# K-features times V in the two halves of the array's columns, with the normalizer's sums added on GpSimd

## The chip, the cores and the metric

The kernel runs on one core of one Trainium2 chip. The metric is the device time of one execution in microseconds; of several executions the median is given. The core's engines are TensorE (matrix products; "PE" in the profile, with "PEld" for the loads of its stationary operand), VectorE (DVE), ScalarE (ACT), GpSimd (POOL) and SyncE (SP), which issues the transfers.

## The reference

Inputs are float32. The attention has 8 batches, 8 heads, 576 tokens and 64 values per head; each head's queries and keys become 256 positive features, and numerator and denominator are linear in them. The result, 4608 tokens by 512, goes through a gated feed-forward with 1536 hidden values.

```python
def phi(x):
    proj = np.einsum('bhsd,df->bhsf', x, w_phi)             # 128 features
    proj = proj - np.max(np.abs(proj), axis=-1, keepdims=True)
    return np.concatenate([np.exp(proj), np.exp(-proj)], axis=-1)
q_p, k_p = (phi(q), phi(k))
kv = np.einsum('bhsf,bhsd->bhfd', k_p, v)
z = np.sum(k_p, axis=2)
num = np.einsum('bhsf,bhfd->bhsd', q_p, kv)
den = np.einsum('bhsf,bhf->bhs', q_p, z)[..., None] + 1e-06
x = num / den                                               # heads side by side: 4608 x 512
out = (sigmoid(x @ w_gate) * (x @ w_val)) @ w_out
```

The change concerns `kv` and `z`: for each head, the sum over tokens of features times values, and the sum over tokens of the features alone.

## The kernel before, in words

The attention runs over 32 pairs of heads (`steps`, 8 batches of 4 pairs). For one pair:

- `load_q`, `load_kv`: transfers of the pair's queries, keys and values. Values come as `vx`, 128 tokens by ten blocks (five blocks of tokens, the two heads alternating) by 65 columns: 64 values and a column of ones, which `layout` puts there. The last block of a head has only 64 tokens; they lie in the partitions of its own half, with zeros in the other.
- `att_k`: the keys' projections on TensorE into `pp` (L316, L321), in three groups `g` (token blocks 0 and 1 of both heads, blocks 2 and 3, and the last half block); VectorE takes the maximum (L325) and subtracts it (L344), ScalarE takes the two exponentials (L350; L338 for the first four pairs). Then the products with V (L358): for each head and each of five token blocks, 65 stationary columns of `vx` by 256 features, in plain float32, added up in `kvp` (65 partitions, 2 heads, 256 features). Row 64 of `kvp` is the sum of the features, because of the column of ones. ScalarE copies `kvp` to `kvt` (L364), TensorE transposes it in four pieces into `tp` (L367), and ScalarE and VectorE copy that out as `kvh` and `kvl` (`split`, L60 and L61), or in the first eight pairs (`WHOLE`) as `kv` (L370).
- `att_q`: the queries' projections (L397, L403) and, on VectorE, their maximum over the features, which lie across the partitions (L413 to L428).
- `att_num`: the queries' exponentials (L439), their splitting (L446, L447) and the products with `kvh` and `kvl` (L456): 65 rows, the last of which is the denominator. Twice per pair, a half of the tokens each.
- `att_norm`, `att_scale`: the reciprocal of the denominator through memory, the scaling (L484) into `xp` (two buffers), and its transfer to `xscr`.

The feed-forward runs in two parts. Its first five blocks of 128 hidden values (`half_units`: L136 into `gv`, L143 into `acc`) run beside the attention, as units that `fill` releases at 0.7 per slot, four slots per pair. The other seven (`rest_chunks`) run when the attention has ended (L136 into `g` and `v`, L143).

The order of the instructions on each engine is not written by hand: the framework lists them with a timeline simulation of its own when the kernel is built; what stands under `attend` has priority over the rest. Each engine then works through its list in order. Memory on the chip is nearly full, which is why many tiles have one or two buffers. Before the change GpSimd makes the identity matrix at the start, and nothing else.

Of the kernel before, what the change touches and what calls it, by code (L numbers as in the profile page):

```python
# [19 lines left out]
F = 128  # L20
# [10 lines left out]
HS = S // 2  # L31
KVW = D + 1

JA = 5  # feed-forward blocks that run beside the attention
JR = 8  # blocks JA to JR - 1 take the attention's bytes, the others phase 1's
WHOLE = 8  # first pairs: plain float32 products, no splits
DIRECT = 4  # first pairs: K's exponentials straight from PSUM
PRIORITY = 400
RATE, LAG = 0.7, 2  # feed-forward units per slot; slots from x to its first unit


@with_exitstack
def attention_moe(
# [20 lines left out]
        for m in marks:  # L64
            stack.enter_context(tc.issue_after(m.ins))

# [1 line left out]
    weights = {}  # L68

    ebias = const.tile([P, 1], F32, name="ebias")  # L70
    vec.memset(ebias, -896.0 * 2.0**23)

    def from_f64(h, l, raw, mid, sp, nb, name):
        # h: the value cut to 12 bits; l: the other bits as an integer times their unit
        words = raw.rearrange("p (n two) -> p n two", two=2)
        lo, hi = words[:, :, 0], words[:, :, 1]
        top = sp.tile([P, DM], U32, tag="wtop", name="wtop" + name, bufs=nb)
        vec.tensor_scalar(top, hi, 0x7FFFFE00, None, op0=ALU.bitwise_and)
        relu = act.activation(top, top, AF.Relu, bias=ebias, scale=8.0)
        vec.scalar_tensor_tensor(  # L80
            top, hi, 0x80000000, top, op0=ALU.bitwise_and, op1=ALU.bitwise_or
        )
        vec.tensor_copy(h, top.bitcast(F32))
        if mid is None:
            rest, unit = hi, lo
            vec.tensor_scalar(
                hi, hi, 16, 0x01FF0000, op0=ALU.logical_shift_left, op1=ALU.bitwise_and
            )
            vec.scalar_tensor_tensor(
                hi, lo, 16, hi, op0=ALU.logical_shift_right, op1=ALU.bitwise_or  # L90
            )
        else:
            words = mid.rearrange("p (n two) -> p n two", two=2)
            rest, unit = words[:, :, 0], words[:, :, 1]
            vec.tensor_scalar(rest, rest, 0x01FFFFFF, None, op0=ALU.bitwise_and)
        vec.tensor_scalar(unit, top, 0xFF800000, None, op0=ALU.bitwise_and)
        return relu, vec.scalar_tensor_tensor(
            l, rest, 2.0**-36, unit.bitcast(F32), op0=ALU.mult, op1=ALU.mult
        )

    def load_weights(j, m, wp, sp, nb, twice):
        if m == 0:
            wh = wp.tile([P, 3 * DM], F32R, tag=f"wh{j}", name=f"wh{j}")
            wl = wp.tile([P, 3 * DM], F32R, tag=f"wl{j}", name=f"wl{j}")
            weights[j] = (wh, wl)
        wh, wl = weights[j]
        ms = slice(m * DM, m * DM + DM)
        raw = sp.tile([P, 2 * DM], U32, tag="wraw", name=f"wraw{j}_{m}", bufs=nb + 1)
        load, mid = nc.sync.dma_start(raw, w_moe[j, :, m, :].bitcast(U32)), None
        if twice:  # L110
            # the same rows two bytes on: a word then holds the bits below h's
            mid = sp.tile([P, 2 * DM], U32, tag="wmid", name=f"wmid{j}_{m}", bufs=nb)
            nc.sync.dma_start(
                mid[:, : 2 * DM - 1].bitcast(U16),
                w_moe[j, :, m, :].bitcast(U16)[:, 1 : 4 * DM - 1],
            )
        return load, *from_f64(wh[:, ms], wl[:, ms], raw, mid, sp, nb, f"{j}_{m}")
# [135 lines left out]
            xs = nxt  # L253
        out_step(*late)

# [1 line left out]
    with ExitStack() as actx:  # L257
        wp1 = actx.enter_context(tc.tile_pool(name="wp1", bufs=1))
        moe = actx.enter_context(tc.tile_pool(name="moe1", bufs=2))
# [5 lines left out]
        ps_n = actx.enter_context(tc.tile_pool(name="ps_n", bufs=1, space=PSUM))  # L265
        ps_acc = actx.enter_context(tc.tile_pool(name="ps_o", bufs=1, space=PSUM))

        ident = at1.tile([KVW, KVW], F32, name="ident")
        make_identity(nc, ident)
        wk = at1.tile([P, 3 * F], F32, name="wk")  # L270
        nc.sync.dma_start(wk, w_phi)
        wq = at1.tile([P, 2, 3 * F], F32R, name="wq")
# [12 lines left out]
        def load_kv(b, p):  # L285
            n = f"{b}_{p}"
            kx = at.tile([P, 5 * P], F32, tag="kin", name="k" + n)
            nc.sync.dma_start(kx, k[b, p])
            vx = at.tile([P, 10, KVW], F32, tag="vin", name="v" + n)
            nc.sync.dma_start(vx, v[b, p])  # L290
            loaded["kv", b, p] = (kx, vx)

        def att_k(b, p):
            n = f"{b}_{p}"
            kx, vx = loaded.pop(("kv", b, p))
            kvp = ps_kv.tile([KVW, 2, 2 * F], F32, tag="kvp", name="kvp" + n)
            es = []
            whole = b * NP + p < WHOLE
            if not whole:
# [3 lines left out]
            for g in range(3):  # L303
# [38 lines left out]
                else:  # L342
# [6 lines left out]
                    for sg in range(2):  # L349
# [2 lines left out]
                            scale=1.0 - 2.0 * sg,  # L352
                        )
                es.append(e)
            for hd in range(2):
                for t in range(5):
                    slot = 2 * t + hd
                    nc.tensor.matmul(  # L358
                        kvp[:, hd, :], vx[:, slot, :],
                        es[t // 2][:, slot % 4 if t < 4 else 0, :],  # L360
                        start=t == 0, stop=t == 4,
                    )
            kvt = at.tile([KVW, 4, F], F32, tag="kvt", name="kvt" + n, bufs=1)
            act.copy(kvt.rearrange("p a f -> p (a f)"), kvp.rearrange("p a f -> p (a f)"))  # L364
            tp = ps_kv.tile([P, 4, KVW], F32, tag="kvp", name="tp" + n)
            for i in range(4):
                nc.tensor.transpose(tp[:, i, :], kvt[:, i, :], ident)  # L367
            if b * NP + p < WHOLE:
                kv = at.tile([P, 4, KVW], F32, tag="kv", name="kv" + n)
                act.copy(kv, tp)  # L370
                kvs[b, p] = (kv,)
            else:
                kvh = at.tile([P, 4, KVW], F32R, tag="kv", name="kvh" + n)
                kvl = at.tile([P, 4, KVW], F32R, tag="kvl", name="kvl" + n)
                split(kvh, kvl, tp)
                kvs[b, p] = (kvh, kvl)

        def att_q(b, p):
# [53 lines left out]
        def att_num(b, p, hf):  # L432
            n = f"{b}_{p}_{hf}"
            d, ex = qst[b, p]
            cs = slice(hf * HS, hf * HS + HS)
            terms = []
            for sg in range(2):
                e = at.tile([P, 2, HS], F32, tag="eq", name=f"eq{n}_{sg}", bufs=2)
                act.activation(e, d[:, :, cs], AF.Exp, scale=1.0 - 2.0 * sg)  # L439
                if len(kvs[b, p]) == 1:  # L440
                    terms.append([(kvs[b, p][0], e)])
                else:
                    kvh, kvl = kvs[b, p]
                    eh = at.tile([P, 2, HS], F32R, tag="eqh", name=f"eqh{n}_{sg}", bufs=2)
                    el = at.tile([P, 2, HS], F32R, tag="eql", name=f"eql{n}_{sg}", bufs=2)
                    act.copy(eh, e)  # L446
                    late[b, p, hf, sg] = vec.tensor_tensor(  # L447
                        el, e, eh.bitcast(F32), op=ALU.subtract
                    )
                    terms.append([(kvh, eh), (kvl, eh), (kvh, el)])  # L450
            for hd in range(2):
                nm = ps_n.tile([KVW, HS], F32, tag="nm", name=f"nm{n}_{hd}")
                last = len(terms[0]) - 1
                for sg in range(2):
                    for i, (a, x) in enumerate(terms[sg]):
                        nc.tensor.matmul(  # L456
                            nm, a[:, 2 * hd + sg, :], x[:, hd, :],
                            start=sg == 0 and i == 0, stop=sg == 1 and i == last,
                        )
                act.copy(ex[:, hd, cs], nm)  # L460
# [18 lines left out]
        def att_scale(b, p):  # L479
            n = f"{b}_{p}"  # L480
            ex, rb = rbs.pop((b, p))
            xp = at.tile([P, S], F32, tag="xp", name="xp" + n, bufs=2)
            for hd in range(2):
                vec.tensor_tensor(  # L484
                    xp[hd * D : hd * D + D, :], ex[0:D, hd, :], rb[:, hd, :], op=ALU.mult
                )
            t = 0
            while t < S:
                c, o = divmod(b * S + t, CH)
                w = min(CH - o, S - t)  # L490
                nc.sync.dma_start(
                    xscr[c][:, p * CH + o : p * CH + o + w], xp[:, t : t + w]
                )
                t += w
# [104 lines left out]
def layout(inputs):  # L599
    import numpy as np  # L600

    def feature_major(x):
# [5 lines left out]
    kt[:, :, :D, 4 * P : 4 * P + D] = x[:, :, :D, 4 * P :]  # L608
    kt[:, :, D:, 4 * P + D :] = x[:, :, D:, 4 * P :]
    x = inputs["v"].reshape(B, NP, 2, S, D)  # L610
    x = np.concatenate([x, np.ones_like(x[..., :1])], axis=-1)
    vt = np.zeros((B, NP, P, 10, KVW), x.dtype)
    vt[:, :, :, :8] = (
        x[:, :, :, : 4 * P]
        .reshape(B, NP, 2, 4, P, KVW)
        .transpose(0, 1, 4, 3, 2, 5)
        .reshape(B, NP, P, 8, KVW)
    )
    vt[:, :, :D, 8] = x[:, :, 0, 4 * P :]
    vt[:, :, D:, 9] = x[:, :, 1, 4 * P :]  # L620
# [17 lines left out]
```

## Time and profile before

| | us |
|---|---|
| median of 3 executions | 1304.68 |
| lowest, highest | 1303.23, 1305.15 |
| profiled execution, span from first to last instruction | 1307.2 |
| TensorE busy in it | 1269.8 |
| VectorE busy | 877.5 |
| ScalarE busy | 650.7 |
| GpSimd busy | 0.6 |

The profile is of one execution, whose span is given in the table. "L358" is line 358 of the kernel before. In a row of grouped instructions stand the line, the engine, the operation, the program's names for what is written and read, the shapes, the count, the busy time in us, the mean duration of one in ns, and the idle time of the engine ahead of them with what ended it. A matmul's duration is modelled and overlaps its neighbours'; the distance from one start to the next is what it takes of the engine. The chain of waits is followed back from the last instruction, at each step to what released it or to the instruction before it on its engine; a piece of it such as "x10" holds ten instructions one behind the other. In tables by stretch of time, each engine's busy time stands with its number of instructions.

### The profile page before, as it was taken

The numbers are of one execution on the slowest core, as the hardware profiler recorded it, in microseconds if no ns is written. First come the engines' busy times: TensorE is split into PE (matmuls) and PEld (weight loads), VectorE is DVE, ScalarE is ACT, GpSimd is POOL, SyncE is SP. The second block draws the span as 40 slices with busy tenths as digits, with TensorE's granted clock in tenths as the row PEclk, the third lists the DMA queues.
The fourth block names the chain that finished last, engine by engine and source line by source line (L and its number), as shares of the span: only waits on it lengthen the run. The fifth ranks groups of instructions, "written<-read, shape, count | busy, mean of one in ns | idle before, by whom it ended". The sixth has DMA issues, their size and how long they took to land.

```text
span 1307.2 us, 19107 instructions
## 1 busy us (share of the span) xinstructions
PE 1269.8 (97%) x7112; PEld 1070.8 (82%) x7112; DVE 877.5 (67%) x1778; ACT 650.7 (50%) x1416; POOL 0.6 (0%) x6
## 2 busy tenths in 40 slices
PE   7878999999999999999999999999999999999998
PEld 4545788999898989898998988888888888888886
DVE  5777989899899888989866958834343443434333
ACT  5754777777777787777754523322222222222221
POOL 0000000000000000000000000000000000000000
PEclk9988999999999999999999999999999999999999
DMA  5576543233233323332225424313021211202010
GB/s 190 165 216 195 167 131 100 85 107 105 86 115 86 107 84 118 94 108 76 61 69 180 130 78 132 97 65 97 1 97 33 65 50 48 97 1 97 1 65 33
DMA packets 75166, 125.12 MB, mean 96 GB/s; under 512 B 18496, under 2 KB 38080, under 8 KB 75072
## 3 DMA queue, kind: packets, MB, share of 16 engines
q1 hardware_dynamic: 75072, 123.89, 30.7%
q8 instruction: 56, 0.92, 0.3%
q14 instruction: 38, 0.31, 0.1%
HBM read 95.25 MB, written 28.46 MB: 95 GB/s over the span
## 4 chain that ended last, share of the span: by engine, by line
PE 88%; DVE 4%; DMA 4%; ACT 2%; issue 1%; SPq 0%; DVEq 0%; ACTq 0%
PE acc L143 22%; PE gv L136 17%; PE g L136 13%; PE v L136 13%; PE kvp L358 9%; PE nm L456 7%; PE pk L316 3%; PE pq L403 2%; PE pq L397 1%; DMA xs<-xp 1%; DMA q<-q 1%; DMA rb<-den 1%; DMA dn<-ex 1%; ACT ek L338 1%; DMA wraw<-w_moe 1%
## 5 line engine op out<-in xcount | busy, mean ns | idle before, releaser
L136 PE MATMUL gv<-xh,wh 128*128 128x256 f32 x720 | 208.3, 290 | 3.6 <-DVE t L156 3.4
L136 PE MATMUL gv<-xh,wl 128*128 128x256 f32 x720 | 206.5, 287 | 0.0
L136 PE MATMUL gv<-xl,wh 128*128 128x256 f32 x720 | 206.2, 286 | 0.0
L60 ACT CAST hh<-u 128x256 fp32r<-128x256 f32 (+1 forms) x153 | 75.4, 494 | 245.3 <-DVE u L157 245.1
L143 PE MATMUL acc<-wh,hh 128*128 128x512 f32 x432 | 171.3, 397 | 0.7 <-ACT y L187 0.7
L143 PE MATMUL acc<-wl,hh 128*128 128x512 f32 x432 | 169.9, 393 | 0.0
L143 PE MATMUL acc<-wh,hl 128*128 128x512 f32 x432 | 166.1, 394 | 0.1
L358 PE MATMUL kvp<-ek,v 128*65 128x256 f32 x640 | 158.6, 383 | 6.9 <-ACT ek L338 5.3
L155 DVE TENSOR_SCALAR t<-t 128x256 uint32<-128x256 uint32 (+1 forms) x153 | 52.5, 344 | 154.6 <-ACT t L152 153.7
L136 PEld LDWEIGHTS gv<-xh,wh 128*128 128x128 f32 x720 | 137.1, 191 | 10.0 <-DVE t L156 4.7
L136 PEld LDWEIGHTS gv<-xl,wh 128*128 128x128 f32 x720 | 137.0, 190 | 3.3
L136 PEld LDWEIGHTS gv<-xh,wl 128*128 128x128 f32 x720 | 137.0, 190 | 2.3
L358 PEld LDWEIGHTS kvp<-ek,v 128*65 128x65 f32 x640 | 86.6, 138 | 49.4 <-ACT ek L338 9.7
L61 DVE TENSOR_TENSOR hl<-u,hh 128x256 fp32r<-128x256 f32 (+1 forms) x153 | 81.1, 531 | 47.2 <-ACT hh L60 46.1
L152 ACT ACTIVATE t<-g 128x512 f32<-128x512 f32 x63 | 37.6, 597 | 150.0 <-PE g L136 149.8
L156 DVE SCALAR_TENSOR_TENSOR t<-t,v 128x512 f32<-128x512 f32 x63 | 43.3, 687 | 85.6 <-PE v L136 85.4
L136 PE MATMUL g<-xh,wh 128*128 128x512 f32 x252 | 99.0, 393 | 0.0
L136 PE MATMUL v<-xh,wh 128*128 128x512 f32 x252 | 98.6, 391 | 0.0
L136 PE MATMUL g<-xl,wh 128*128 128x512 f32 x252 | 98.6, 391 | 0.0
L136 PE MATMUL g<-xh,wl 128*128 128x512 f32 x252 | 98.5, 391 | 0.0
L136 PE MATMUL v<-xl,wh 128*128 128x512 f32 x252 | 98.3, 390 | 0.0
L136 PE MATMUL v<-xh,wl 128*128 128x512 f32 x252 | 98.2, 390 | 0.0
(91 smaller groups left out, 2533.6 us busy)
## 6 DMA issues: line engine op xcount, KB each, us to landing
wraw<-w_moe SPq DMA_DIRECT2D x36, 512.0 KB, 3.9
xl<-xs SPq DMA_DIRECT2D x36, 512.0 KB, 4.1
v<-v SPq DMA_DIRECT2D x32, 325.0 KB, 3.3
k<-k SPq DMA_DIRECT2D x32, 320.0 KB, 3.1
q<-q SPq DMA_DIRECT2D x32, 288.0 KB, 3.2
rb<-den SPq DMA_DIRECT2D x32, 288.0 KB, 3.8
ys<-y SPq DMA_DIRECT2D x36, 256.0 KB, 2.1
yp<-ys SPq DMA_DIRECT2D x36, 256.0 KB, 4.3
```

Of the source, the lines that this page charges most:

```text
L60: a = act.copy(h, x)
L61: return a, vec.tensor_tensor(l, x, h.bitcast(F32), op=ALU.subtract)
L136: nc.tensor.matmul(o, a[:, ws], x[:, cs], start=i == 0, stop=i == 11)
L143: nc.tensor.matmul(acc, a[:, ts], w[:, ws], start=first and i == 0, stop=last and i == 2)
L152: act.activation(t, g, AF.Tanh, scale=0.5)
L155: vec.tensor_scalar(tu, tu, 0x7FFFFFFF, None, op0=ALU.bitwise_and)
L156: vec.scalar_tensor_tensor(t, t, 1.0, vl, op0=ALU.add, op1=ALU.mult)
L316: nc.tensor.matmul(o, x[:, ts], w, start=t == 0, stop=t == len(terms) - 1)
L338: act.activation(e[:, i, sg * F : sg * F + F], pp[:, i, :], AF.Exp, bias=(mn, mx)[sg][:, i : i + 1], scale=1.0 - 2.0 * sg,)
L358: nc.tensor.matmul(kvp[:, hd, :], vx[:, slot, :], es[t // 2][:, slot % 4 if t < 4 else 0, :], start=t == 0, stop=t == 4,)
L403: nc.tensor.matmul(pp, wq[:, i, 2 * F :], s[:, hd, cs], start=i == 0, stop=i == 1,)
L456: nc.tensor.matmul(nm, a[:, 2 * hd + sg, :], x[:, hd, :], start=sg == 0 and i == 0, stop=sg == 1 and i == last,)
```

## The change

The values lose their column of ones, so a head's product has 64 stationary columns. Head 0's goes to partitions 0 to 63 of `kvp`, head 1's to partitions 64 to 127, of the same 256 columns; the loops over token blocks and heads change places, so that the heads alternate. The sums of the features over the tokens are now made in two steps: GpSimd adds the exponentials of a head's token blocks elementwise into `su` (128 partitions by 2 heads by 256), and two products with a matrix of ones add up the 128 partitions, into the other half of `kvp`, where each of 64 partitions then holds the same sum.

```diff
-        ident = at1.tile([KVW, KVW], F32, name="ident")
+        ident = at1.tile([P, P], F32, name="ident")
         make_identity(nc, ident)
+        ones = at1.tile([P, D], F32, name="ones")
+        vec.memset(ones, 1.0)
...
-            vx = at.tile([P, 10, KVW], F32, tag="vin", name="v" + n)
+            vx = at.tile([P, 10, D], F32, tag="vin", name="v" + n)
...
-            kvp = ps_kv.tile([KVW, 2, 2 * F], F32, tag="kvp", name="kvp" + n)
+            kvp = ps_kv.tile([P, 2, 2 * F], F32, tag="kvp", name="kvp" + n)
...
+            su = at.tile([P, 2, 2 * F], F32, tag="su", name="su" + n, bufs=1)
+            pool.tensor_tensor(su, es[0][:, 0:2, :], es[0][:, 2:4, :], op=ALU.add)
+            for i in (0, 2):
+                pool.tensor_tensor(su, su, es[1][:, i : i + 2, :], op=ALU.add)
             for hd in range(2):
-                for t in range(5):
+                own = slice(hd * D, hd * D + D)
+                pool.tensor_tensor(
+                    su[own, hd, :], su[own, hd, :], es[2][own, 0, :], op=ALU.add
+                )
+
+            for t in range(5):
+                for hd in range(2):
                     slot = 2 * t + hd
                     nc.tensor.matmul(
-                        kvp[:, hd, :], vx[:, slot, :],
+                        kvp[hd * D : hd * D + D, 0, :], vx[:, slot, :],
                         es[t // 2][:, slot % 4 if t < 4 else 0, :],
                         start=t == 0, stop=t == 4,
                     )
-            kvt = at.tile([KVW, 4, F], F32, tag="kvt", name="kvt" + n, bufs=1)
+            for hd in range(2):
+                nc.tensor.matmul(
+                    kvp[hd * D : hd * D + D, 1, :], ones, su[:, hd, :],
+                    start=True, stop=True,
+                )
+            kvt = at.tile([P, 4, F], F32, tag="kvt", name="kvt" + n, bufs=1)
             act.copy(kvt.rearrange("p a f -> p (a f)"), kvp.rearrange("p a f -> p (a f)"))
-            tp = ps_kv.tile([P, 4, KVW], F32, tag="kvp", name="tp" + n)
+            tp = ps_kv.tile([P, 4, P], F32, tag="kvp", name="tp" + n)
             for i in range(4):
                 nc.tensor.transpose(tp[:, i, :], kvt[:, i, :], ident)
+            parts = [
+                (slice(0, D), tp[:, 0:2, :].rearrange("p s (h d) -> p h s d", h=2)),
+                (
+                    slice(D, KVW),
+                    tp[:, 2:4, :].rearrange("p s (h d) -> p h s d", h=2)[:, :, :, 0:1],
+                ),
+            ]
...
-                split(kvh, kvl, tp)
+                for ds, x in parts:
+                    split(kvh[:, :, :, ds], kvl[:, :, :, ds], x)
...
-            xp = at.tile([P, S], F32, tag="xp", name="xp" + n, bufs=2)
+            xp = at.tile([P, S], F32, tag="xp", name="xp" + n, bufs=1)
```

`kv`, `kvh` and `kvl` now have the shape 128 by 2 heads by 2 signs by 65, L456 takes its pieces by head and sign, and `layout` leaves out the column of ones. The order of the tokens in `vx`, the rest of the attention and the feed-forward stay as they are.

More of the change, by code (lines that the diff above doesn't have):

```diff
@@ L362, in att_k @@
                     )
-            kvt = at.tile([KVW, 4, F], F32, tag="kvt", name="kvt" + n, bufs=1)
+            for hd in range(2):
[4 more added lines that the diff above has]
+            kvt = at.tile([P, 4, F], F32, tag="kvt", name="kvt" + n, bufs=1)
             act.copy(kvt.rearrange("p a f -> p (a f)"), kvp.rearrange("p a f -> p (a f)"))
-            tp = ps_kv.tile([P, 4, KVW], F32, tag="kvp", name="tp" + n)
+            tp = ps_kv.tile([P, 4, P], F32, tag="kvp", name="tp" + n)
             for i in range(4):
                 nc.tensor.transpose(tp[:, i, :], kvt[:, i, :], ident)
+            parts = [
[5 more added lines that the diff above has]
+            ]
             if b * NP + p < WHOLE:
-                kv = at.tile([P, 4, KVW], F32, tag="kv", name="kv" + n)
-                act.copy(kv, tp)
+                kv = at.tile([P, 2, 2, KVW], F32, tag="kv", name="kv" + n)
+                for ds, x in parts:
+                    act.copy(kv[:, :, :, ds], x)
                 kvs[b, p] = (kv,)
             else:
-                kvh = at.tile([P, 4, KVW], F32R, tag="kv", name="kvh" + n)
-                kvl = at.tile([P, 4, KVW], F32R, tag="kvl", name="kvl" + n)
-                split(kvh, kvl, tp)
+                kvh = at.tile([P, 2, 2, KVW], F32R, tag="kv", name="kvh" + n)
+                kvl = at.tile([P, 2, 2, KVW], F32R, tag="kvl", name="kvl" + n)
+                for ds, x in parts:
+                    split(kvh[:, :, :, ds], kvl[:, :, :, ds], x)
                 kvs[b, p] = (kvh, kvl)
@@ L456, in att_num @@
                         nc.tensor.matmul(
-                            nm, a[:, 2 * hd + sg, :], x[:, hd, :],
+                            nm, a[:, hd, sg, :], x[:, hd, :],
                             start=sg == 0 and i == 0, stop=sg == 1 and i == last,
@@ L610, in layout @@
     x = inputs["v"].reshape(B, NP, 2, S, D)
-    x = np.concatenate([x, np.ones_like(x[..., :1])], axis=-1)
-    vt = np.zeros((B, NP, P, 10, KVW), x.dtype)
+    vt = np.zeros((B, NP, P, 10, D), x.dtype)
     vt[:, :, :, :8] = (
         x[:, :, :, : 4 * P]
-        .reshape(B, NP, 2, 4, P, KVW)
+        .reshape(B, NP, 2, 4, P, D)
         .transpose(0, 1, 4, 3, 2, 5)
-        .reshape(B, NP, P, 8, KVW)
+        .reshape(B, NP, P, 8, D)
     )
```

## The prediction

> **What bounds the kernel now.** I read the page's parts 1, 2 and 4 first.
>
> ```profile
> span 1307.2 us, 19107 instructions
> PE 1269.8 (97%) x7112; PEld 1070.8 (82%) x7112; DVE 877.5 (67%) x1778; ACT 650.7 (50%) x1416; POOL 0.6 (0%) x6
> PE   7878999999999999999999999999999999999998
> DVE  5777989899899888989866958834343443434333
> PE 88%; DVE 4%; DMA 4%; ACT 2%; issue 1%; SPq 0%; DVEq 0%; ACTq 0%
> PE acc L143 22%; PE gv L136 17%; PE g L136 13%; PE v L136 13%; PE kvp L358 9%; PE nm L456 7%; PE pk L316 3%; PE pq L403 2%; PE pq L397 1%; DMA xs<-xp 1%; DMA q<-q 1%; DMA rb<-den 1%; DMA dn<-ex 1%; ACT ek L338 1%; DMA wraw<-w_moe 1%
> ```
>
> TensorE is 88% of the chain that ended last, and K-features times V (L358) is 9% of it. But 97% and 67% are averages over stages, so I cut the span at 172 us (the eight WHOLE pairs end about there), 694 (attention ends) and 782 (the feed-forward alone). Columns: stretch, length, busy time (instructions) of PE, weight loads, DVE, ACT, POOL.
>
> ```profile
> 0.00:172.00 172.00, 143.27 (x675) 97.70 (x676) 134.20 (x302) 107.47 (x270) 0.60 (x6) 0.95 0.59 185
> 172.00:694.00 522.00, 521.84 (x3596) 469.98 (x3597) 451.09 (x952) 377.47 (x859) 0.00 (x0) 1.00 0.32 94
> ...
> PE gv L136 <- DVE t L156: 1.6, 2, 1.4
> ```
>
> The stage that matters is 172 to 694: 24 pairs in 522 us, 21.75 us each, and TensorE is busy for 521.84. The last line is the longest wait of its matmuls there (1.6 us in all). Nothing else holds the stage, so a microsecond of array time there is a microsecond of the end. VectorE is idle for 522 - 451 = 71 us, 2.96 us a pair: the next bound, not far off. Before 172, TensorE is idle for 29 of 172 us, so there I count array time at half: 24 + 8/2 = **28 pairs' worth**.
>
> **The L358 products.** A busy matmul's duration is not what it costs; its step is. The chain of waits gives the steps of one pair (start, length, piece):
>
> ```profile
> 306.74 1.19 PE gv L136 x10
> ...
> 308.71 0.86 PE kvp L358 x4
> ...
> 310.53 0.86 PE kvp L358 x4
> ...
> 313.40 2.16 PE kvp L358 x10
> ...
> 317.14 0.43 PE kvp L358 x2
> ...
> 321.50 0.24 PE tp L367 x4
> ```
>
> ```profile
> L358 PE MATMUL kvp<-ek,v 128*65 128x256 f32 x640 | 158.6, 383 | 6.9 <-ACT ek L338 5.3 <-ACT ek L350 1.1 <-DMA q<-q 0.4
> L358 PEld LDWEIGHTS kvp<-ek,v 128*65 128x65 f32 x640 | 86.6, 138 | 49.4 <-ACT ek L338 9.7 <-ACT ek L350 2.2 <-issue 1.2
> L367 PE MATMUL tp<-ident,kvt 65*128 65x65 f32 x128 | 13.2, 224 | 0.0
> ```
>
> 2.16/10 = 0.216 us per record. The program has 32 x 10 such products and the trace 640 records: a float32 product is two records, one behind the other. A pair pays 20 x 0.216 = **4.32 us**, in four runs (4, 4, 10, 2 records) with other products between them, since the exponentials come in three groups. Each record takes 0.383 us though the step is 0.216: 0.167 us of its depth lies under its neighbours. The 65-column weight load of 0.138 us is under the step too.
>
> **What the change does to TensorE.**
>
> *Removed by overlap.* The heads' products now use 64 columns each, in two halves, and alternate. No product before the change uses half of the columns, so no row shows whether two run at once; the bounds are a step of 0.216 per record (none) and per two records (full). In favour, from rows: gv takes 256 float32 columns per 0.119 us, so operands can stream at nearly twice L358's rate; two L358 streams would need 0.216 for two, against 2 x 0.119 = 0.238. I take overlap at 0.216.
>
> But the order is head 0 first record, second record, head 1 first, second. The two records of one head use the same half and can't overlap each other. So a run of n records takes n/2 + 1 steps: the first and the last have one half empty.
>
> *Added.* Two products with `ones`: four records. So there are 24. The order by token block makes runs of 8 (first group), 8 (second), 4 (third) and 4 (the sums, which come from GpSimd): 5 + 5 + 3 + 3 = 16 steps, 16 x 0.216 = 3.46. Against 4.32 that is **-0.86 us a pair**. If the third group joins the second (12 records), 15 steps and -1.08.
>
> *Transposes.* 0.24/4 = 0.06 us for 65 columns; 128 columns cost at least that and at most 128/65 of it, 0.118: between 0 and +0.23 a pair. I take **+0.12**, the middle.
>
> *The edges.* Four runs have eight edges between full-width and half-width products. If the array can't hold both kinds at once, the depth that now lies under the neighbour is paid at each edge. Lower bound 0: in the pieces above the edge between kvp and gv costs nothing now. Upper: 0.167 and, if the next weights can't be loaded ahead either, 0.138 more. I take 0.167 at each, the only row that shows the depth: 8 x 0.167 = **+1.34 us a pair**. It decides the sign: the saving is gone from (0.86 - 0.12)/8 = 0.09 us an edge on.
>
> The Trainium skill's page "TensorEngine Tiling (Array Packing)", Key Properties, speaks against the change here: changing the tiling mode, not merely the tile, drains the engine; the same list says that tiles execute in parallel. By that rule the sum is the one with the edges; without it, the one without. No run so far shows which.
>
> Sum for TensorE: -0.86 + 0.12 + 1.34 = +0.60 a pair, x 28 = **+17 us**.
>
> **The other engines.**
>
> ```profile
> masks.py:199 POOL TENSOR_SCALAR_AFFINE_SELECT ident<-ident 65x65 f32<-65x65 f32 x1 | 0.2, 238 | 0.1
> L157 DVE SCALAR_TENSOR_TENSOR u<-u,t 128x512 f32<-128x512 f32 x63 | 43.5, 691 | 5.1
> ...
> 309.42 0.51 ACT L350 ACTIVATE ek<-dk 128x128 f32<-128x128 f32 x2
> ...
> 318.52 0.60 ACT L364 COPY kvt<-kvp 65x512 f32<-65x512 f32 x1
> ```
>
> *GpSimd's adds:* three of 128x512 and two of 64x256. No row shows one. Nearest below: VectorE's 0.69 us for 512 elements; above: GpSimd's own 0.238 us for 65 elements, 1.87 for 512. With half for 256 elements, 4 x 0.69 = 2.8 to 4 x 1.87 = 7.5 us a pair; I take 4 x 1.3 = 5 (middle). What waits is the `ones` product, and in TensorE's order everything behind it. Cover: the third group's exponentials end at 309.42 + 0.51 = 309.9, the last L358 product of that pair at 317.14 + 0.43 = 317.6. Even 7.5 us from about 306, when the first group is there, end at 313.5. The buffers of the exponentials, which GpSimd now holds too, and the one of the sums are wanted again a pair later. Cost 0; if the product is placed where the data are ready instead, up to 3.6 us a pair.
>
> *The copies:* kvt keeps its 512 elements per partition (0.60 us); the tp copies become a long and a small one.
>
> ```profile
> L335 DVE TENSOR_SCALAR mn<-mx 128x4 f32<-128x4 f32 x8 | 1.1, 160 | 0.0
> L350 ACT ACTIVATE ek<-dk 128x128 f32<-128x128 f32 x56 | 14.3, 304 | 1.3 <-DVE dk L344 1.1
> xs<-xp SPq DMA_DIRECT2D x48, 128.0 KB, 1.8
> ```
>
> The small one costs at most 0.3 us on ScalarE (nearest row 128x128) and 0.16 on VectorE, both inside their idle time: 0. `xp` with one buffer waits for pieces that land 1.8 us after issue and is written a pair (21.75 us) later: 0. V's load loses 5 of 325 KB: 0. SP's and GpSimd's queues get no new transfer. The larger identity and `ones` are made once: 0.
>
> *VectorE beside GpSimd.* GpSimd has done nothing so far; what its adds do to VectorE no row shows. Bounds: 0, and, where the two can't read at once, all of GpSimd's time that meets such an instruction of VectorE (two operands from SBUF). The rows of these:
>
> ```profile
> L447 DVE TENSOR_TENSOR eql<-eq,eqh 128x576 fp32r<-128x576 f32 x96 | 70.2, 752 | 11.0 <-ACT eqh L446 9.6 <-PE pq L403 1.2
> L388 DVE TENSOR_TENSOR sq<-q,sq 64x576 fp32r<-64x576 f32 x48 | 36.1, 753 | 1.5
> L428 DVE TENSOR_TENSOR d<-d,mb 128x1152 f32<-128x1152 f32 x32 | 43.3, 1353 | 0.3
> L484 DVE TENSOR_TENSOR xp<-ex,rb 64x576 f32<-64x576 f32 x64 | 47.9, 749 | 10.9 <-DMA rb<-den 10.4
> L61 DVE TENSOR_TENSOR kl<-k,kh 128x512 fp32r<-128x512 f32 x24 | 16.4, 682 | 0.1
> ```
>
> With three quarters of L428 and L484 (24 of 32 pairs) these are 70.2 + 36.1 + 32.5 + 35.9 + 16.4 = 191 us of the stage's 522, 37%. A loss of 0.37 x 5 = 1.9 us a pair fits the 2.96 that VectorE has free: 0. With 7.5 it is 2.8, and the small copy's 0.16 fills it to the brim.
>
> The Trainium skill's page "SBUF — State Buffer", section "Who interferes with whom", says more: VectorE with two SBUF inputs and a GpSimd instruction that reads SBUF exclude each other for the whole instruction. By that rule the 1.9 us are real; no trace so far shows it.
>
> **The sum.** 1307.2 + 17 = 1324 us of span. The median is 1304.68, 2.5 below that execution's span, so about **1321 us**, 1.3% slower.
>
> **The rivals.**
>
> *A, faster: overlap, and edges that cost next to nothing.* -0.74 us a pair, x 28 = -21: **1284**. If the empty halves at the edges are filled too (12 steps), 2.59 - 4.32 + 0.12 = -1.61, x 28 = -45: 1260. It decides below 0.09 us an edge. For it: kvp next to gv costs nothing now. Against: both use the whole array now.
>
> *B, the forecast.* With half of the depth at each edge, -0.07 a pair: 1303; with the weight load on top, +1.7: 1352.
>
> *C, the change doesn't do what it says: no overlap.* 24 records one by one, +0.86 + 0.12 = +0.98, x 28 = +27: **1332**; with the transposes at their upper bound and all 32 pairs, +35: 1340.
>
> *D, VectorE becomes the bound or the sums come late.* If it loses more than 2.8 us a pair, the stage follows it: each microsecond beyond is 24 us at the end. At GpSimd's upper 7.5 us and with the feed-forward's two-operand steps added (half of VectorE's time in place of 37%) 3.75 + 0.16 - 2.96 = +0.95, 23 us: **1328**; with a `ones` product that waits a microsecond as well, 1352.
>
> **Chances.** A 0.33; B 0.37, of which 0.09 lie near half depth; C 0.18; D 0.12. The measurement can tell 0.2% (2.6 us) from no change. Faster 0.33, same 0.09, slower 0.28 (the rest of B) + 0.18 + 0.12 = 0.58. The range: 1278 leaves out the far part of A (0.09), 1346 the tops of B and D (0.09). B alone would be 1303 to 1340.
>
> **What would show it.** Starts of L358's records: two within one step of 0.216 (overlap) or one (C). Between a run of them and the next gv: 0.12 us (A) or 0.17 more (B). TensorE's waits in the stage: still about none, or on GpSimd (D); VectorE's mean durations at L447 and L388: 0.75, or longer (D). TensorE's part of the stage shorter than 522 us is A. A wrong depth or a different number of runs would break the forecast first.

## The result and the profile after

| | before | after |
|---|---|---|
| median, us | 1304.91 | 1385.72 |
| ratio, 95% interval | | 1.0615 [1.0597, 1.0634] |
| span of the profiled execution, us | 1307.2 | 1383.6 |

The kernel before ran once more beside the changed one, hence its 1304.91. The change costs 81 us (6%). The forecast was 1321 us, slower by 16, with a range up to 1346: right in its sign, five times too small. After the change L358's products stand at L371, the products with ones at L377, the adds at L359, L361 and L364; L422, L428, L447 and L456 have become L449, L455, L474 and L483.

The page of the changed kernel, parts 1, 2 and 4:

```profile
span 1383.6 us, 19743 instructions
PE 1305.1 (94%) x7240; PEld 1045.0 (76%) x7240; DVE 977.1 (71%) x1803; ACT 652.4 (47%) x1448; POOL 196.9 (14%) x166
DVE  6889998988988999999996595972434434334333
PE 62%; DVE 24%; issue 5%; ACT 4%; DMA 4%; POOL 0%; SPq 0%; DVEq 0%; ACTq 0%; POOLq 0%
```

GpSimd is busy for 197 us, and VectorE for 100 us more than before (877 to 977), though only the small copies out of `tp` and one fill were added to its list. It now holds 24% of the chain that ended last (4% before) and TensorE 62% (88%). The table by stretch, for the attention's steady stage, which now lasts until 758:

```profile
172.00:758.00 586.00, 551.81 (x3697) 451.63 (x3694) 531.15 (x994) 384.05 (x892) 144.16 (x118) 0.97 0.28 85
```

586 us in place of 522. TensorE is idle for 34 of them, where it was idle for 0.2; VectorE is busy for 531, 91%, where it was 86%. The other 12 us of the longer span stand at the end: the stretch with the feed-forward alone takes 537.6 us, where it took 525.2, with 65 more of TensorE's records left for it. The waits of TensorE in the stage that add up to most (total us, times, longest):

```profile
PE nm L483 <- DVE eql L474: 9.8, 7, 4.4
PE gv L136 <- DVE t L156: 6.1, 6, 1.8
PE nm L483 <- DVE kvl L61: 4.5, 2, 2.5
```

Of the 34 us, 22 are waits for VectorE and 11 for ScalarE. Where VectorE's time went is seen in the timeline of VectorE, GpSimd and TensorE (start, length, in us):

```profile
315.71 1.40 DVE L155 TENSOR_SCALAR t<-t 128x256 uint32<-128x256 uint32 x1
...
317.34 1.52 DVE L157 SCALAR_TENSOR_TENSOR u<-u,t 128x256 f32<-128x256 f32 x1
...
319.42 1.72 DVE L449 COPY pn<-pm 32x36 f32<-32x36 f32 x4
...
322.76 0.74 DVE L474 TENSOR_TENSOR eql<-eq,eqh 128x576 fp32r<-128x576 f32 x1
```

```profile
315.67 1.29 POOL L359 TENSOR_TENSOR su<-ek 128x512 f32<-128x512 f32 x1 [17.08 <-ACT ek L352]
317.29 2.70 POOL L361 TENSOR_TENSOR su<-su,ek 128x512 f32<-128x512 f32 x2 [0.33 <-ACT ek L352]
```

```profile
316.64 1.95 PE L371 MATMUL kvp<-ek,v 128*64 128x256 f32 x16
318.63 0.34 PE L483 MATMUL nm<-eqh,kvh 128*65 128x288 f32 x1
318.81 0.29 PE L483 MATMUL nm<-eqh,kvl 128*65 128x288 f32 x1
323.55 0.43 PE L483 MATMUL nm<-eql,kvh 128*65 128x288 f32 x1 [4.45 <-DVE eql L474]
```

The same two shapes in the kernel before, and the small copies, grouped by line:

```profile
L155 DVE TENSOR_SCALAR t<-t 128x256 uint32<-128x256 uint32 x90 | 25.6, 287 | 19.1 <-ACT t L152 18.4
L157 DVE SCALAR_TENSOR_TENSOR u<-u,t 128x256 f32<-128x256 f32 x90 | 37.6, 420 | 1.2
L422 DVE COPY pn<-pm 32x36 f32<-32x36 f32 x128 | 22.3, 174 | 2.4
```

L155 starts 0.04 us after an add and ends 0.15 us after it; it takes 1.40 us, where this shape took 0.287 on average. L157 does the same at the next add: 1.52 in place of 0.42. The four copies at L449 take 1.72, where four at 0.174 are 0.70. A few microseconds on, TensorE stands still for 4.45 us, waiting for a result of VectorE (L474) that stands in its list behind these. The same block shows the half that the forecast hoped for: 16 records with 64 columns take 1.95 us, where 16 full-width steps of 0.216 are 3.46.

The same wait and the time right behind it, as stretches (the columns as above, then the granted clock, the share of the transfers' engines and GB/s):

```profile
319.10:323.55 4.45, 0.01 (x1) 0.00 (x0) 4.35 (x11) 1.93 (x6) 2.87 (x3) 1.00 0.01 1
323.70:327.10 3.40, 3.40 (x12) 1.77 (x11) 3.40 (x6) 2.08 (x4) 0.00 (x0) 0.50 0.00 0
```

VectorE is busy for 4.35 of the 4.45 us. Behind the wait TensorE's granted clock is 0.50 for 3.4 us; over the stage it is 0.97, where it was 1.00, and over the whole 0.981, where it was 0.992. The span times the missing share gives an estimate of what the clock takes: 26 us after and 10 before, so some 16 of the 76 us of longer span. No run tests whether the waits alone bring the clock down.

### The profile page after: what moved, and what is told of

Same layout as the page of the kernel before. It is cut to its first block, busy times and chain, and to the rows that moved or that the text cites. A ratio compares the mean times of both kernels' runs of the same rounds, so it can differ in the third digit from the quotient of the medians.

```text
span 1383.6 us, 19743 instructions
## 1 busy us (share of the span) xinstructions
PE 1305.1 (94%) x7240; PEld 1045.0 (76%) x7240; DVE 977.1 (71%) x1803; ACT 652.4 (47%) x1448; POOL 196.9 (14%) x166
## 4 chain that ended last, share of the span: by engine, by line
PE 62%; DVE 24%; issue 5%; ACT 4%; DMA 4%; POOL 0%; SPq 0%; DVEq 0%; ACTq 0%; POOLq 0%
PE acc L143 17%; PE g L136 13%; PE v L136 12%; PE gv L136 9%; PE nm L483 4%; PE kvp L371 3%; DVE pn L449 2%; DVE mx L327 2%; DVE pm L440 2%; DVE eql L474 2%; DVE dk L346 1%; PE kvp L377 1%; PE pk L318 1%; DVE xp L511 1%; DVE d L455 1%
## 5 line engine op out<-in xcount | busy, mean ns | idle before, releaser
L155 DVE TENSOR_SCALAR t<-t 128x256 uint32<-128x256 uint32 (+1 forms) x153 | 57.2, 374 | 155.3 <-ACT t L152 154.6
L61 DVE TENSOR_TENSOR hl<-u,hh 128x256 fp32r<-128x256 f32 (+1 forms) x153 | 84.4, 552 | 51.6 <-ACT hh L60 49.8
L359 POOL TENSOR_TENSOR su<-ek 128x512 f32<-128x512 f32 x32 | 47.1, 1471 | 476.9 <-ACT ek L352 402.7
L371 PE MATMUL kvp<-ek,v 128*64 128x256 f32 x640 | 106.9, 425 | 2.4 <-ACT ek L340 1.6
L466 ACT ACTIVATE eq<-d 128x576 f32<-128x576 f32 x128 | 85.5, 686 | 38.5 <-DVE eql L474 17.9
```

The source lines that it names most:

```text
L61: return a, vec.tensor_tensor(l, x, h.bitcast(F32), op=ALU.subtract)
L155: vec.tensor_scalar(tu, tu, 0x7FFFFFFF, None, op0=ALU.bitwise_and)
L359: pool.tensor_tensor(su, es[0][:, 0:2, :], es[0][:, 2:4, :], op=ALU.add)
L371: nc.tensor.matmul(kvp[hd * D : hd * D + D, 0, :], vx[:, slot, :], es[t // 2][:, slot % 4 if t < 4 else 0, :], start=t == 0, stop=t == 4,)
```

## The experiments

Theory T: GpSimd's adds hold VectorE up while they read, and the attention's stage then waits for VectorE. Rivals: the half-width products cost the time (R), or the sums' place in the plan does (O). All kernels were run beside the kernel before; medians in us.

**The parts alone: e1, e2, e15**

```diff
e1_no_adds: the changed kernel
-            (su and its five adds)
...
-                    kvp[hd * D : hd * D + D, 1, :], ones, su[:, hd, :],
+                    kvp[hd * D : hd * D + D, 1, :], ones, es[2][:, 0, :],
e2_adds_alone: the kernel before
+            (su and its five adds on GpSimd, ahead of L355)
e15_tiny_adds: as e2, on one column per head
+            pool.tensor_tensor(su[:, :, 0:1], es[0][:, 0:2, 0:1], es[0][:, 2:4, 0:1], op=ALU.add)
...
```

> The changed kernel without GpSimd's five adds; the products with ones read the last group's exponentials, so the sums over tokens are incomplete and the rest of the work is the same. Theory T (GpSimd's adds hold VectorE up, and VectorE becomes the bound of the attention): the loss goes and TensorE's gain shows. In the changed kernel 16 records in a row take 1.99 us where 16 steps of 0.216 are 3.46, so 24 records cost about 24 x 0.108 + 4 x 0.2 for the edges = 3.4 us a pair against 4.32; with +0.1 for the wider transposes that is -0.8 x 28 = -22: 1283 us, VectorE's busy time back at 880. Rival R (the halves and their edges cost the time): 1360 to 1385, as with the adds.

> The kernel before with GpSimd's five adds put in and nothing made of their result (xp with one buffer, to make room). T: VectorE's busy time rises from 877 to about 975 us and the whole to 1370 to 1400. R: 1303 to 1308, nothing waits for GpSimd here.

> The kernel before with GpSimd's five adds a pair at the same places, each of one column per head in place of 256: the same instructions and waits, hardly any work. Theory T (what costs is the time for which GpSimd reads and VectorE is held): GpSimd's busy time under 50 us, VectorE's 877 to 895, the whole 1300 to 1325. Rival (five more instructions in the plan, with another order of everything, cost it, whatever their length): 1360 to 1390 as with the full adds.

| | median | ratio to before, 95% |
|---|---|---|
| e1_no_adds | 1318.14 | 1.0094 [1.0061, 1.0126] |
| e2_adds_alone | 1385.31 | 1.0614 [1.0594, 1.0634] |
| e15_tiny_adds | 1309.51 | 1.0028 [1.0015, 1.0041] |

The adds alone, in the kernel before and with their result unused, cost all that the change costs. With the same five instructions at the same places but hardly any length, 4 us are left, though GpSimd is still busy for 56 us (under 50 was expected). So it is neither the halves nor the plan but the length of the adds. The pages of e2 and e15, part 1, then the rows for the adds' first, the two-operand split and the small copies, of e2:

```profile
PE 1295.0 (94%) x7112; PEld 1075.7 (78%) x7112; DVE 977.7 (71%) x1778; ACT 648.4 (47%) x1416; POOL 198.0 (14%) x166
```

```profile
PE 1272.1 (97%) x7112; PEld 1072.7 (82%) x7112; DVE 879.3 (67%) x1778; ACT 646.7 (49%) x1416; POOL 56.1 (4%) x166
```

```profile
L456 DVE TENSOR_TENSOR eql<-eq,eqh 128x576 fp32r<-128x576 f32 x96 | 80.7, 865 | 13.1 <-ACT eqh L455 11.4 <-PE pq L412 0.7 <-PE tp L376 0.4
L431 DVE COPY pn<-pm 32x36 f32<-32x36 f32 x128 | 54.1, 423 | 2.3
L356 POOL TENSOR_TENSOR su<-ek 128x512 f32<-128x512 f32 x32 | 46.4, 1451 | 486.4 <-ACT ek L350 446.7 <-ACT ek L338 39.7
```

VectorE has the same 1778 instructions in all three (before, e2, e15) and needs 877.5, 977.7 and 879.3 us. The split went from 752 to 865 ns, the copies of 32x36 from 174 to 423.

e1's own forecast failed: 1283 was expected, 1318 came. Without adds VectorE is back at 881 us, yet the halves bring nothing. Its granted clock, 0.988, takes some 5 us more than before by the estimate above. What becomes of the overlap is told with e9.

**How much, and by what: e5, e6**

```diff
e5_half_adds: the kernel before, three adds a pair, of 128x256
+            pool.tensor_tensor(su[:, 0:1, :], es[0][:, 0:1, :], es[0][:, 2:3, :], op=ALU.add)
...
e6_memset: the kernel before
                     for sg in range(2):
                         act.activation(...)
+                    for _ in range(5 if g < 2 else 0):
+                        pool.memset(dk, 0.0)
```

> The kernel before with three adds of 128x256 a pair on GpSimd, nothing made of them: in elements 3 x 256 of the 4 x 512 that the five adds have. Theory T (VectorE loses time in proportion to GpSimd's reading): GpSimd's busy time about 75 us in place of 198, VectorE's 877 + 0.38 x 100 = 915; as VectorE has 71 us to spare in the stage, the whole loses less than in proportion: 1308 to 1335. Rival (any add in the list spoils the order): 1370 or more.

> The kernel before with GpSimd writing and not reading: ten memsets of 128x512 a pair over the differences dk after ScalarE has read them (in the 28 pairs that have dk), GpSimd busy for some 150 us. If GpSimd's reading is what holds VectorE's two-operand instructions up, L447 and L428 keep their 752 and 1353 ns; if the copies and the instructions with one operand and a scalar are held up by writes too, L422 and L155 grow as they did (174 to 420, 287 to 338 ns): 1306 to 1325. If any work of GpSimd takes as much as the adds: 1365 or more and L447 at 820 or more.

Measured: e5 1317.86 (1.0094 [1.0079, 1.0109]), e6 1329.08 (1.0178 [1.0161, 1.0195]); e6 lies just above its bound of 1325. Part 1 of e5's page, then groups of e6 (L449, L424 and L430 are L447, L422 and L428 before):

```profile
PE 1274.7 (97%) x7112; PEld 1072.1 (82%) x7112; DVE 910.0 (69%) x1778; ACT 647.8 (49%) x1416; POOL 84.7 (6%) x102
```

```profile
L355 POOL MEMSET dk<- 128x512 f32 x280 | 144.8, 542 | 531.3 <-ACT ek L350 507.4 <-DVE mx L325 17.0
L449 DVE TENSOR_TENSOR eql<-eq,eqh 128x576 fp32r<-128x576 f32 x96 | 69.8, 752 | 5.7 <-ACT eqh L448 4.3 <-PE pq L405 0.3
L424 DVE COPY pn<-pm 32x36 f32<-32x36 f32 x128 | 53.1, 415 | 2.3
L430 DVE TENSOR_TENSOR d<-d,mb 128x1152 f32<-128x1152 f32 x32 | 43.1, 1347 | 0.3
L155 DVE TENSOR_SCALAR t<-t 128x256 uint32<-128x256 uint32 x90 | 30.8, 344 | 10.5 <-ACT t L152 9.9
```

VectorE's loss grows with the adds' length, but it isn't a fixed share of GpSimd's busy time: 2 us for 56 (e15), 33 for 85 (e5), 100 for 198 (e2). The whole's loss grows faster still: 4 us, 12, then 79. In e6 GpSimd only writes, and VectorE's instructions with two operands keep their 752 and 1347 ns. The copies are held as long as under the adds (415), and so are L155's instructions with one operand and scalars (344; 287 before, 338 after the change). So reading is what holds these two-operand instructions, while adds and memsets both hold the copies and L155. The Trainium skill's page "SBUF — State Buffer", section "Who interferes with whom", says just that: two-input VectorE instructions contend with GpSimd instructions that read, not with those that only write, and copies in a two-port mode with any; these rows agree on both, though none shows the copies' mode.

**The adds on VectorE itself: e3**

```diff
-            pool.tensor_tensor(
+            vec.tensor_tensor(
```

> The changed kernel with the five adds on VectorE. They cost it 4 x 0.69 = 2.8 us a pair; it has 2.96 to spare before the change. T: 1285 to 1330, faster than with GpSimd by over 50, though the same engine does more. Rival O (the sums come late, whoever makes them, and the order listed around them is worse): 1350 or more.

Measured 1369.66 (1.0497 [1.0467, 1.0528]), 16 us faster than on GpSimd (over 50 was expected) and 40 above the expected range's end: inside rival O's range. The products with ones wait for the sums for 1.6 us in all, so late sums are not it; whether the order is worse was not tested. The part of the theory that VectorE can take up to its idle time for nothing does not hold here: 77 us more of VectorE's busy time than in e1 (958.4 against 881.4) come with 52 more of the whole. Part of that is the clock: 0.975 in the profiled execution, against 0.988, by the estimate above some 18 of the 58 us between the two spans. Still, five adds cost VectorE less when it makes them than when GpSimd does (77 against 96 us, both over e1).

**Taking work off VectorE: e7, e8, e13, e14**

```diff
e7_after_less_vector, e8_before_less_vector
-            marks.append(vec.tensor_tensor(d, d, mb, op=ALU.subtract))
+            marks.append(vec.tensor_tensor(d[:, :, 0:1], d[:, :, 0:1], mb[:, :, 0:1], op=ALU.subtract))
e13_copies_scalar (changed kernel), e14_before_copies (kernel before)
-                vec.tensor_copy(pn[a * 32 : a * 32 + 32], pm[o * 32 : o * 32 + 32])
+                act.copy(pn[a * 32 : a * 32 + 32], pm[o * 32 : o * 32 + 32])
```

> The changed kernel with VectorE's subtraction of the queries' maximum cut from 1152 columns to 2 (the exponentials that follow are of unscaled values). VectorE does 32 x 1.3 = 42 us less. T (VectorE bounds the attention stage in the changed kernel): 1386 falls by 25 to 50, to 1336 to 1361. Rival: under 10 us gained.

> The kernel before with the same cut. T (TensorE bounds it there): 1296 to 1307, next to nothing. Rival (VectorE bounds it already): 1265 to 1285.

> The changed kernel with the four small copies between partitions (L449, 32x36, four a pair) on ScalarE, which has time to spare; nothing else differs. In the changed kernel these 128 copies take VectorE 53.8 us, where the same copies took 22.3 before: the difference is waiting for GpSimd. T (VectorE's time, lost to GpSimd, is what the attention stage waits for): VectorE's busy time falls by about 50 us and the whole by 20 to 45, to 1341 to 1366. Rival (the late sums or the order): 1380 or more.

> The control: the kernel before with the same four copies on ScalarE. They cost VectorE 22.3 us there and it has time to spare. T: 1298 to 1315, no gain beyond what another order gives. If VectorE's time counts there as well: under 1290.

| | median | against its own kernel |
|---|---|---|
| e7, changed kernel | 1370.35 | -15 |
| e8, kernel before | 1313.59 | +8 |
| e13, changed kernel | 1372.55 | -13 |
| e14, kernel before | 1323.75 | +18 |

In the changed kernel less work on VectorE helps, in the kernel before it doesn't: that VectorE has become what the stage waits for holds in its sign. In size both e7 and e13 fell short of their expectations (25 and 20 us at least). Two things stand against a plain reading. In e13 VectorE's busy time fell by 32 us, not 50: GpSimd then holds other instructions (the splits of the queries at L415 go from 810 to 1007 ns). And e8 and e14 both end above their ranges: the kernel before loses 8 and 18 us though VectorE has less to do. The likely reason, not shown, is that the planner lists everything anew; single differences of that size, e7's and e13's too, say little here.

**The halves without the adds: e9, e10, e4**

```diff
e9_one_run (from e1), e10_before_one_run (from the kernel before)
-                for t in range(5):
+                for t in (4, 0, 1, 2, 3):
...
-                        start=t == 0, stop=t == 4,
+                        start=t == 4, stop=t == 3,
```

> e1_no_adds with the last token block first in the accumulation, so that all 24 half-width records of a pair stand in one run (the sums over tokens are incomplete, as there). Theory E (the overlap is real, and what eats it are the many short runs: 115 in e1, each with some 0.2 us of edges, and 23 of them with one head alone): a run of 24 takes 12 x 0.216 + 0.2 = 2.8 us, about 0.9 less than e1's 117 us / 32 = 3.7; x 28 = -25: 1318 falls to 1285 to 1300, under the kernel before. Rival (the array's time no longer bounds it): 1310 or more.

> The control: the kernel before with the last token block first, so that its 20 full-width records stand closer together. E: edges cost nothing there, 1300 to 1312. If longer runs alone shorten the whole: under 1295.

Measured: e9 1319.28 (1.0106 [1.0087, 1.0125]), e10 1330.87 (1.0191 [1.0165, 1.0217]). Both miss their ranges, and e9 alone would have spoken for its rival; but with the same order of token blocks the halves are 12 us faster. Why e10 loses 25 us was not found. TensorE's timeline around a run, in the kernel before, in e1 and in e9:

```profile
308.41 0.29 PE L456 MATMUL nm<-eqh,kvl 128*65 128x288 f32 x1
308.54 1.03 PE L358 MATMUL kvp<-ek,v 128*65 128x256 f32 x4
309.22 0.47 PE L136 MATMUL gv<-xh,wh 128*128 128x256 f32 x1
309.53 0.29 PE L456 MATMUL nm<-eql,kvh 128*65 128x288 f32 x1
```

```profile
309.36 0.34 PE L474 MATMUL nm<-eql,kvh 128*65 128x288 f32 x1
309.63 1.52 PE L362 MATMUL kvp<-ek,v 128*64 128x256 f32 x12
311.08 0.39 PE L136 MATMUL gv<-xh,wl 128*128 128x256 f32 x1
311.30 0.28 PE L136 MATMUL gv<-xh,wh 128*128 128x256 f32 x1
```

```profile
332.13 0.28 PE L136 MATMUL gv<-xl,wh 128*128 128x256 f32 x1
332.34 2.38 PE L362 MATMUL kvp<-ek,v 128*64 128x256 f32 x20
334.55 0.60 PE L368 MATMUL kvp<-ek,ones 128*64 128x256 f32 x4
335.08 0.39 PE L136 MATMUL gv<-xh,wl 128*128 128x256 f32 x1
335.30 0.28 PE L136 MATMUL gv<-xh,wh 128*128 128x256 f32 x1
```

From the start of the product ahead of a run to that of the second one behind it: before, 309.53 - 308.41 = 1.12 us, of which 0.13 + 4 x 0.216 + 0.12 = 1.11 are steps: the edges cost nothing. In e1 1.94, of which 0.13 + 6 x 0.216 + 0.12 = 1.55 are steps (12 records, two at a time): 0.39 for the two edges. In e9 3.17 against 0.12 + 12 x 0.216 + 0.12 = 2.83: 0.34, for 24 records. Reckoned like this over the whole trace, e1 has 115 runs: the median run of 8 records pays 0.35 us, the 23 runs of a single product 0.60 (its two records don't overlap), some 53 us together. Runs of three products pay 0.59 as well: the odd product is alone for a step. Added to 768 x 0.108 = 83 us of steps that is 136, against 640 x 0.216 = 138 before: **the edges eat the overlap**, and the wider transposes come on top. e9 has 62 runs and some 32 us of edges: 115 us, 23 less than before. That the whole doesn't gain them is in part the clock (0.983, some 12 us more than before by the estimate above); the rest is open.

The e4 kernel makes K's exponentials stationary and needs neither halves nor adds:

```diff
+            for hd in range(2):
+                for sg in range(2):
+                    for t in range(5):
+                        slot = 2 * t + hd
+                        nc.tensor.matmul(
+                            tp[:, 2 * hd + sg, :],
+                            es[t // 2][:, slot % 4 if t < 4 else 0, sg * F : sg * F + F],
+                            vx[:, slot, :], start=t == 0, stop=t == 4,
+                        )
```

> Another way to the change's end, from the kernel before: K's exponentials are the stationary operand (128 columns) and V with its column of ones the moving one (65 columns), so the result comes out already transposed; the copy to kvt and the transposes go, and no adds are needed. 40 records a pair. If the 128-column load hides as it does at the transposes (0.061 us a step), 40 x 0.061 = 2.4 us against 4.32 + 0.24: -2.1 x 28 = -59, 1246 us. If a float32 load of 0.138 us does not hide under 65 columns: 5.5 us a pair, +1 x 28, 1332.

Measured 1322.89 (1.0138 [1.0097, 1.0179]). Its group of products:

```profile
L359 PE MATMUL tp<-v,ek 128*128 128x65 f32 x1280 | 170.3, 278 | 8.6 <-ACT ek L349 3.9 <-ACT ek L337 3.9 <-DMA k<-k 0.6
```

1280 records keep TensorE busy for 170.3 us, 5.3 us a pair and not the 2.4 hoped for. The median step is 0.112 us, where the transposes had 0.061: the 128-column load does not seem to hide under 65 columns here, but no run tests the load by itself. The time lies between the two forecasts.

## Why the prediction was right in its sign and wrong in its size

**What bounds the kernel before:** right. TensorE does (e8, e14: less work on VectorE gains nothing).

**Overlap at 0.216 us for two records:** right. **n/2 + 1 steps in a run:** wrong for the runs that were assumed. The two heads' records pair up from the first one on, so a run with an even number of products takes n/2 steps: e1's run of 12 lasts 1.52 us, five steps and one duration of 0.43. The four runs would have taken 12 steps and not 16, -1.73 us a pair in place of -0.86. Runs with an odd number of products do pay the step more.

**0.167 us at each edge:** right; two edges cost 0.34 to 0.39 in the rows above, 0.35 in the median run of 8. The Trainium skill's rule of the drain at a change of mode ("TensorEngine Tiling (Array Packing)", Key Properties) agrees with them. **Four runs a pair:** 115 in e1 and 146 after, for the 128 assumed; 59 of the 146 are a single product. **Transposes at 0.12 us a pair:** near the upper bound: four of them take 0.60 in the row below, less one duration of 0.27 (273 ns in the group's mean) over three steps, 0.109 each, +0.2.

```profile
306.08 0.60 PE L385 MATMUL tp<-ident,kvt 128*128 128x128 f32 x4
```

TensorE's sum was +0.60 us a pair. e1 pays (136 - 138)/32 + 0.2 = +0.14; e1's 12 us over the kernel before are more than that. The clock's 5 us are part of them, and the rest is of a size that another order alone can make (e8, e10, e14); which part is order was not settled. In the changed kernel the runs are shorter, their edges come to 67 us or more in the same reckoning, and the sum to some (83 + 67 - 138)/32 + 0.2 = +0.6: the forecast's figure, but by luck: each even run takes fewer steps than reckoned, and there are more runs, many of them odd.

**GpSimd's adds, 5 us a pair between 2.8 and 7.5:** 197/32 = 6.2, in the bounds. **Hidden sums:** right on the whole; TensorE's matmuls at L377 waited 0.5 us for GpSimd in all:

```profile
L377 PE MATMUL kvp<-su,ones 128*64 128x256 f32 x128 | 36.4, 410 | 0.5 <-POOL su L364 0.5
```

**The step that failed** is "A loss of 1.9 us a pair fits the 2.96 that VectorE has free: 0". It was wrong twice. The loss is 100/32 = 3.1 us a pair (e2): only instructions with two operands from SBUF outside the feed-forward were counted, and not the copies, whose 128 small ones alone lose 31.5 us, nor L155 and L157. The five rows that were counted lose 25 us, 0.8 a pair, less than the 1.9 reckoned. And idle time doesn't absorb such a loss. e3 puts 77/32 = 2.4 us a pair on VectorE, less than is free, and the whole is 52 us longer; e5 takes 33/32 = 1.0 from it and is 12 longer, though 12 is of the size that another order can make. Each engine works its list in order, so what is late on VectorE stops TensorE, as in the 4.45 us above, during which VectorE was busy throughout. That the other waits come about in the same way is argued from the table of waits and not followed one by one. Rival D had the mechanism, with a chance of 0.12, and priced it with the same threshold, at 1328 to 1352.

## What to carry to other kernels

Before work goes to an idle GpSimd, count VectorE's instructions that read two operands from SBUF, and its copies, over the stage in which GpSimd will read: in this kernel the full adds took 100 us from VectorE in their 198, the shorter ones 33 in 85, and under the full ones the end paid most of it (79). Count half-width products by runs, not by records: each run costs two edges, so the halves save TensorE's steps only where many products of both heads stand together, and e9's whole was no faster even then. Idle time of an engine that feeds the bound is no budget when all lists are in order; test the price with the added work alone, its result unused, and again with the same instructions made tiny.

## What the hardware showed that was not expected

A float32 product is two records, and the records of products in the two halves run side by side from the first on: 24 records in 12 steps. Five adds on GpSimd cost VectorE more (96 us over e1) than the same five adds do when VectorE makes them (77 us). A copy of 32x36 that takes VectorE 0.17 us lasts just as long beside memsets of GpSimd as beside its adds (415 and 423 ns on average). Behind a wait of 4.45 us TensorE's granted clock was 0.50 for 3.4 us, so a wait can cost more than its length.
